# The late chunks' vector, scalar and Pool work in the source's order, transposes one slot later, and the second projection's weights in two arrays

## The chip, the cores and the metric

One core of one Trainium2 chip runs the kernel. The metric is the device time of one execution in microseconds. Before the change it is 664.35 us, the median of three runs (664.12 to 664.52).

## The reference

A banded attention with a linear position bias, followed by a two-layer feed-forward net without residual. B = 4, H = 8, S = 768, D = 64; a query sees 8 global keys and the 96 keys up to itself. q, k and v are float32, the two weights float64.

```python
scores = scale * np.matmul(q, k.transpose(0, 1, 3, 2))
keep = is_global | is_local                  # pos < 8, or 0 <= rel < 96
bias = -slopes[:, None, None] * dist[None, :, :]
scores = np.where(keep, scores + bias[None, :, :, :], -1000000000.0)
a = np.exp(scores - np.max(scores, axis=-1, keepdims=True))
a = a / (np.sum(a, axis=-1, keepdims=True) + 1e-09)
x = np.matmul(a, v)                          # then [B, S, H*D] -> 3072 x 512
h = x @ w_in                                 # 512 -> 2048
g = np.maximum(0.01 * h, h)
return (g @ w_out).astype(np.float32)        # 2048 -> 512
```

## The kernel before

**Tiling.** The 3072 tokens are 24 steps of 128. The attention of a step is two *units* of four heads each, 48 units in all. The feed-forward net takes *chunks* of steps: two of three steps, then nine of two (`CHUNKS`). Every float32 factor of the net is kept as a high part, rounded to TensorE's fp32r, and a remainder; each product is three matmuls (high x high, high x low, low x high). `copy` to fp32r on ACT makes the high part (`gh`, L511), a subtraction on DVE the low one (`gl`, L513).

**An attention unit** passes through *events*. Event t runs on TensorE the product with v of unit t-2 (L346) and the scores of unit t (L205). ACT copies the former from PSUM (`x`, L352), Pool splits it into the net's input. DVE adds the bias and takes the row's extreme (L219), ACT takes the exponential with its row sum (L232), DVE adds 1e-9 to the sum and inverts it (`rs`, L253 and L254), ACT scales the rows by it (L261). From unit 14 on the probabilities are then turned without TensorE (`turn`, L274): a DVE transpose of 32 x 32 blocks in place (L278), a DMA to a DRAM tile `via` (L243), and four DMAs back into `pt_d` (L245), all issued on the sync queue SP. Event t+2 reads `pt_d`.

**The early part** works through chunks 0 and 1 with attention events and the conversion of the weights between them. **The late loop** (L671 to L688) does the other nine chunks in 72 slots, eight for each chunk, a slot being a pair of the 16 blocks of 128 hidden units. In slot s stand, as written: the events of the slot (in slots 0, 1, 3 and 5 of eight, four for each chunk: those of the following chunk), `hidden_pair(s)` (24 matmuls, L491), `gates(s)`, `turn` of the slot's units, and `out_pair(s-2)`, the second projection of two slots ago (L542). `gates` copies the hidden pair from PSUM (`t`, L502), issues the fetch of a weight tile of the first projection for slot s+2 into a ring of two (`ring`, L479, on ACT's queue; it must wait until the tile's last reader is done), takes the leaky maximum (L504), makes the four block sums of a seven-product scheme (L507), and `gh` and `gl`; in the first chunks it also prepares the scheme's sums of `wout` (`prepare`, L523 and L601). From the third late chunk on (`SEVEN`) seven of a chunk's eight slots, all but the first, run with seven products in place of eight. At a chunk's end `results` copies three PSUM banks (L567, L572, L573), combines them on DVE (L523) and stores two rows of 128 x 512.

The hidden pair of odd slots uses the bank `ps_p`; its second half is also one of the four output banks (L666), so that the next output pair waits for the copy of `t`.

**What sets the order.** TensorE's instructions always keep the order of the source (`keep_in_program_order`). Those of DVE, ACT and Pool do so where `pin` is called while `pinned[0]` is true; `pinned[0] = j < half + NF` (L632) leaves it false at the end of the early part, so in the late loop these three engines are ordered by the scheduler, which simulates a time line (L1027) and takes what it deems ready. DMA issues on SP and on ACT's queue are left to the scheduler everywhere.

Of the kernel before, what the change touches and what calls it, by code (L numbers as in the profile page):

```python
# [11 lines left out]
F32R = mybir.dt.float32r  # L12
# [6 lines left out]
P = 128  # L19
# [33 lines left out]
def fast_path(ctx, tc, qp, kp, vp, wi, wo, nvec, nmall, out, B, H, S):  # L53
    nc = tc.nc
    NB = S // P
    DM = H * D
    NK = DM // P
    NF = wi.shape[0]
# [5 lines left out]
    GT = P * PAIR  # L64
# [3 lines left out]
    ring = ctx.enter_context(tc.tile_pool(name="ring", bufs=RING))  # L68
    win.update({2 * n + 1: ring.tile([P, 2, NK, P], F32R, name="ring") for n in range(RING)})
    outer = ctx.enter_context(tc.tile_pool(name="outer", bufs=1))  # L70
    wout = outer.tile([P, NF, 2, DM], F32R, name="wout")

    const = ctx.enter_context(tc.tile_pool(name="const", bufs=1))
    raw = ctx.enter_context(tc.tile_pool(name="raw", bufs=2))
# [41 lines left out]
    pinned = [True]  # L116
# [8 lines left out]
    def conversion(p):  # L125

        m, f = pieces[p]
        to = wout[:, f] if m else win[f]
        dh, dl = to[:, 0], to[:, 1]
        load_piece(p + STAGES - 1)  # L130
        scale, shift, low, *parts = split_float64(tc, pin, stage, staged.pop(p), dh, dl)
        due.extend(parts)
        return scale, shift, low

    units = {}
    NUNIT = NSTEP * NU
# [112 lines left out]
    def sums(u):  # L249
        d = units[u]  # L250
        sm = d.pop("sm")
        rs = att.tile([P, 16], F32, name="rs")[:, :4]
        pin(nc.vector.tensor_scalar(out=rs, in0=sm, scalar1=1e-9, scalar2=None, op0=ALU.add))  # L253
        pin(nc.vector.reciprocal(out=rs, in_=rs))  # L254
        if u >= BY_DVE:
            pr = d["pr"]
            for a in range(2):
                for j in range(2):
                    p, n = head(u, pr, a, j), 2 * a + j
                    if late.get("a"):  # L260
                        pin(nc.scalar.activation(out=p, in_=p, func=AF.Copy, scale=rs[:, n:n + 1]))  # L261
                    else:
                        pin(nc.vector.tensor_scalar(out=p, in0=p, scalar1=rs[:, n:n + 1], scalar2=1.0, op0=ALU.mult,
                                                    op1=ALU.mult))
            if not late.get("a"):
                turn(u)
            return

        dg = kept_rows.tile([P, 4, HALF], F32, name="dg")
        pin(nc.gpsimd.tensor_tensor(out=dg, in0=eye.unsqueeze(1).to_broadcast([P, 4, HALF]),  # L270
                                    in1=rs.unsqueeze(2).to_broadcast([P, 4, HALF]), op=ALU.mult))
        d["dg"] = dg
# [94 lines left out]
        pin(copy_exact(nc.gpsimd, xh, x))  # L367
        pin(nc.gpsimd.tensor_tensor(out=xl, in0=x, in1=xh.bitcast(F32), op=ALU.subtract))

    def event(t, conv=()):  # L370

        now, mid, old = t < NUNIT, t - 1 in units, t - 2 in units
        if t < LEAD + 2:

            av = (ps_lead if t % 2 else ps_x).tile([P, 2, 512], F32, tag="ps_av", name="ps_sc")
            scores(t, av)
            if mid:
                transposes(t - 1)
            if old:
                ov = ps_lead.tile([P, 2, 512], F32, tag="ps_ov", name="ps_ov")  # L380
                attn_v(t - 2, ov)
        else:

            ov = av = ps_x.tile([P, 2, 512], F32, tag="ps_av", name="ps_av")
            attn_v(t - 2, ov)
            if now:
                scores(t, av)
            if mid:
                transposes(t - 1)
            keep_x(t - 2, ov)  # L390
        if t + 2 < NUNIT:
            load_qk(t + 2)
        if t < NUNIT:
            load_v(t)
        if t < STAGES - 3:
            load_piece(t + 2)
        ends = due[:]
        due.clear()
        if ends:
            ends[0]()  # L400
        scale, shift, low = conversion(conv[0]) if conv else [lambda: None] * 3
        scale()
        if now:
            biased(t, av)
            exps(t)
        if ends:
            ends[1]()
        shift()
        if now:
            sums(t)  # L410
        low()
        if mid:
            keep_pt(t - 1)
        if old and t < LEAD + 2:
            keep_x(t - 2, ov)
        if old:
            split_x(t - 2)
# [10 lines left out]
    def ffn2(j):  # L428
        c, f = order[j]
        gh, gl = gts.pop(j)  # L430
        first = j == 0 or order[j - 1][0] != c
        last = j + 1 == len(order) or order[j + 1][0] != c
        if first:
            acc[c] = [ps_o.tile([P, DM], F32, tag="ps_o", name="ps_o") for _ in range(CHUNKS[c])]
        for tt in range(CHUNKS[c]):
            project(tc, acc[c][tt], wout[:, f], gh, gl, tt, first, last)
        if not last:
            return
        o = acc.pop(c)
        for tt in range(CHUNKS[c]):  # L440
            if f < NF - 1:
                kept.append(kept_rows.tile([P, DM], F32, name="kept", bufs=CHUNKS[c]))
                pin(nc.scalar.copy(out=kept[-1], in_=o[tt]))
                continue
            if c == 0:
                ob = kept[tt]
                nc.vector.tensor_tensor(out=ob, in0=o[tt], in1=ob, op=ALU.add)
            else:
                ob = stage.tile([P, DM], F32, tag="stage", name="part", bufs=STAGES)
                if tt % 2:  # L450
                    nc.vector.tensor_copy(out=ob, in_=o[tt])
                else:
                    nc.scalar.copy(out=ob, in_=o[tt])
            r0 = (first_step[c] + tt) * P
            nc.sync.dma_start(out=out[r0:r0 + P, :], in_=ob)
# [70 lines left out]
        return bank[1 + n // 2][:, n % 2 * GT:(n % 2 + 1) * GT]  # L526

    def block(f, n):
        return tuple(wout[:, f, y, n * GT:(n + 1) * GT] for y in range(2))

    def out_pair(s):

        c, p = at(s)
        gh, gl, a0 = pair.pop(s)

        def times(o, a, bh, bl, first, last, wide=None):
            a -= a0
            for n, (x, y) in enumerate(((gh, bh), (gh, bl), (gl, bh))):
                to = o
                if n == 0 and wide is not None:  # L540
                    to, y = wide
                tc.keep_in_program_order(nc.tensor.matmul(to, lhsT=x[:, a], rhs=y, start=first and n == 0,  # L542
                                                          stop=last and n == 2))
        e, o = 2 * p, 2 * p + 1
        end = s % NP == NP - 1
        if not fast(c, p):
            for n, f in enumerate((e, o)):
                for tt in range(PAIR):
                    times(bank[3 + tt], 2 * n + 1 - tt, wout[:, f, 0], wout[:, f, 1], p + n == 0, end and n == 1)
        else:  # L550
            h, l = sides[p]
            first = p == NP - 1
            t1, t2, t3 = ((h[:, i * GT:(i + 1) * GT], l[:, j * GT:(j + 1) * GT]) for j, i in enumerate((0, 1, 3 if first else 2)))
            for n, a, (bh, bl) in ((0, 5, t2), (1, 1, block(e, 0)), (3, 6, t3), (2, 4, t1), (4, 3, block(o, 0)),
                                   (6, 2, block(e, 1)), (5, 7, block(o, 1))):
                wide = None
                if first and n in (0, 3):
                    wide = bank[1 + n // 2], h[:, (1 + n // 3) * GT:(3 + n // 3) * GT]
                times(half_bank(n), a, bh, bl, wide is not None, end and n in (1, 2, 5, 6), wide)
        if end:  # L560
            results(c)
# [69 lines left out]
    for j in range(len(order)):  # L631
# [36 lines left out]
    sums_at = {2 + n: three[2 * n:2 * n + 2] for n in range(6)}  # L668
    sums_at.update({NP + n: [x] for n, x in enumerate(
        [(3, 0), (3, 1), (7, 3), (6, 3), (5, 3), (4, 3), (3, 2), (3, 3)] + [(p, n) for p in (2, 1) for n in range(4)])})  # L670
    for s in range(NS + 2):  # L671
        for t in ev_pair.get(s, ()):
            event(t)
        if s < NS:
            hidden_pair(s)
        if s == 0:
# [4 lines left out]
            nc.gpsimd.memset(late["w"].tile([P, 16], F32, tag="gap", name="gap"), 0.0)  # L681
        if s < NS:
            gates(s, sums_at.get(s, ()))
        for t in ev_pair.get(s, ()):
            if s and t < NUNIT:
                turn(t)
        if s >= 2:
            out_pair(s - 2)  # L688

# [207 lines left out]
def general_ffn(tc, wi, wo, xs, out):  # L897
# [4 lines left out]
    with ExitStack() as ctx:  # L902
# [14 lines left out]
        with tc.For_i(0, xv.shape[0], 1) as c:  # L917
# [7 lines left out]
            for f in range(NF):  # L925
                gh, gl = hidden(tc, lambda ins: None, work, ps_h, win[:, f], xh, xl, CT)
                for tt in range(CT // P):
                    project(tc, o[:, tt, :], wout[:, f], gh, gl, tt, f == 0, f == NF - 1)
            ob = work.tile([P, CT // P, DM], F32, name="hob")
            nc.scalar.copy(out=ob, in_=o)  # L930
            nc.sync.dma_start(out=ov[bass.ds(c, 1)].rearrange("o (t p) m -> p (o t) m", p=P), in_=ob)
# [25 lines left out]
def project(tc, o, w, gh, gl, tt, first, last):  # L957
    nc = tc.nc
    ts_ = slice(tt * P, (tt + 1) * P)
    tc.keep_in_program_order(nc.tensor.matmul(o, lhsT=gh[:, ts_], rhs=w[:, 0], start=first, stop=False))  # L960
    tc.keep_in_program_order(nc.tensor.matmul(o, lhsT=gh[:, ts_], rhs=w[:, 1], start=False, stop=False))  # L961
    tc.keep_in_program_order(nc.tensor.matmul(o, lhsT=gl[:, ts_], rhs=w[:, 0], start=False, stop=last))  # L962


def tile_kernel(tc, a, out, B, H, S):
# [65 lines left out]
```

## Time and profile before

| | |
|---|---|
| median of three runs | 664.35 us |
| profiled execution | 665.65 us, its span 663.8 us |
| mean granted TensorE clock | 0.977 |
| busy, share of the span | PE 94%, DVE 69%, ACT 52%, POOL 14% |
| waits of ps_p for the copy of t (L542 on L502) | 10.2 us in five waits, the longest 3.9 |
| via, from issue to landing | 3.3 us, 30 transfers |
| pt_d, from issue to landing | 3.5 us, 120 transfers |
| kr, vr, ring, from issue to landing | 4.0, 3.5, 3.4 us |

The page gives for each line of the kernel the busy time of its instructions and the idle time of their engine just before them, with what ended it. A busy TensorE is not TensorE at its peak: the granted clock stands in a row of its own. Timelines list single instructions with their start and length. In them `SPq` and `ACTq` are issues of transfers, whose landing is shown apart. Idle time of an engine that is not waited for costs nothing.

### The profile page before, as it was taken

How to read it: one execution, taken by the hardware profiler on the slowest of the kernel's cores; microseconds unless marked ns; L12 is line 12 of the kernel's file. 1: busy time of each engine (PE TensorE's matmuls, PEld its weight loads, DVE VectorE, ACT ScalarE, POOL GpSimd, SP SyncE). 2: the span in 40 equal slices, each digit the busy share in tenths (PEclk: the TensorE clock that was granted, in tenths of full speed). 3: DMA queues.
4: the chain of work that ended last, by engine and by line, in shares of the span. 5: the costliest groups of instructions: out<-in, count | busy, mean ns of one | idle time of the engine just before them, and what ended most of it. 6: DMA issues, size and time to landing. Idle time of an engine off the chain costs nothing.

```text
span 663.8 us, 16802 instructions
## 1 busy us (share of the span) xinstructions
PE 620.7 (94%) x6536; PEld 569.5 (86%) x6536; DVE 458.2 (69%) x1286; ACT 348.1 (52%) x902; POOL 89.9 (14%) x150
## 2 busy tenths in 40 slices
PE   5679999999999899799979999999999999999993
PEld 4569889998888788689979999999999999999993
DVE  5979988886656974865686676765766766744653
ACT  5877854444444645444545744754664664522321
POOL 3435700000201001000011110110010010110000
PEclk9789999999999999999979999999999999999998
DMA  7775744432547665644745676765765774733311
GB/s 278 242 284 190 222 160 157 157 127 81 166 160 252 206 186 154 201 166 152 242 144 171 192 260 206 213 214 176 231 223 196 227 229 151 229 104 96 127 64 38
DMA packets 63335, 120.71 MB, mean 182 GB/s; under 512 B 8976, under 2 KB 28432, under 8 KB 63248
## 3 DMA queue, kind: packets, MB, share of 16 engines
q1 hardware_dynamic: 53168, 82.86, 38.7%
q10 hardware_dynamic: 10080, 36.70, 16.7%
q8 instruction: 53, 0.87, 0.6%
q14 instruction: 34, 0.28, 0.1%
HBM read 96.21 MB, written 23.33 MB: 180 GB/s over the span
## 4 chain that ended last, share of the span: by engine, by line
PE 75%; DVE 11%; ACT 5%; DMA 4%; issue 2%; POOL 1%; SPq 0%; ACTq 0%; DVEq 0%; POOLq 0%
PE ps_m L542 19%; PE ps_h L491 13%; PE ps_p L491 13%; PE ps_p L542 6%; PE ps_av L346 4%; PE ps_av L205 3%; ACT pr L232 3%; PE ps_h L940 3%; PE ps_h L942 3%; PE ps_o L960 3%; PE ps_o L961 3%; PE ps_h L941 3%; PE ps_o L962 3%; DVE wk L523 3%; DMA out_dram<-part 1%
## 5 line engine op out<-in xcount | busy, mean ns | idle before, releaser
L511 ACT CAST gh<-t 128x896 fp32r<-128x896 f32 (+1 forms) x72 | 61.9, 859 | 100.1 <-DVE t L507 54.9
L513 DVE TENSOR_TENSOR gl<-t,gh 128x896 fp32r<-128x896 f32 (+1 forms) x72 | 70.6, 981 | 52.0 <-ACT gh L511 51.9
L232 ACT ACTIVATE pr<-pr,nmall 128x192 f32<-128x192 f32 (+1 forms) x192 | 83.3, 437 | 23.7 <-DVE nmall L219 23.5
L49 POOL TENSOR_SCALAR xh<-x 128x256 fp32r<-128x256 f32 x48 | 28.6, 596 | 453.4 <-ACT x L352 370.6
L542 PE MATMUL ps_m<-wout,gh 128*128 128x256 f32 (+1 forms) x394 | 86.9, 302 | 0.0
L504 DVE SCALAR_TENSOR_TENSOR t<-t 128x512 f32<-128x512 f32 x72 | 49.7, 690 | 41.1 <-ACT t L502 40.5
L542 PEld LDWEIGHTS ps_m<-wout,gh 128*128 128x128 f32 x394 | 61.7, 189 | 1.9
L542 PE MATMUL ps_m<-wout,gl 128*128 128x256 f32 (+1 forms) x197 | 59.6, 303 | 0.5 <-DVE gl L513 0.5
L491 PE MATMUL ps_p<-xh,win 128*128 128x256 f32 x288 | 58.2, 287 | 0.0
L491 PE MATMUL ps_h<-xh,win 128*128 128x256 f32 x288 | 58.1, 286 | 0.0
L491 PE MATMUL ps_h<-xh,ring 128*128 128x256 f32 x288 | 56.4, 281 | 0.0
L542 PE MATMUL ps_p<-wout,gh 128*128 128x256 f32 (+1 forms) x182 | 46.3, 336 | 10.3 <-ACT t L502 10.2
L491 PE MATMUL ps_p<-xh,ring 128*128 128x256 f32 x288 | 55.1, 277 | 0.0
L507 DVE TENSOR_TENSOR t<-t 128x128 f32<-128x128 f32 x212 | 52.0, 285 | 2.7
L491 PEld LDWEIGHTS ps_p<-xh,win 128*128 128x128 f32 x288 | 46.3, 188 | 5.9 <-issue 5.7
L219 DVE CUSTOM_DVE_ANT_0 pr<-ps_av,nbw 128x192 f32<-128x192 f32 x136 | 40.3, 352 | 15.7 <-ACT x L352 15.6
L491 PEld LDWEIGHTS ps_h<-xh,win 128*128 128x128 f32 x288 | 47.7, 193 | 2.5 <-issue 2.2
L491 PEld LDWEIGHTS ps_h<-xh,ring 128*128 128x128 f32 x288 | 47.1, 191 | 0.0
L491 PEld LDWEIGHTS ps_p<-xh,ring 128*128 128x128 f32 x288 | 46.2, 188 | 0.0
L542 PE MATMUL ps_m<-h,gh 128*128 128x256 f32 (+1 forms) x159 | 46.1, 290 | 0.0
L261 ACT ACTIVATE pr<-pr,rs 128x192 f32<-128x192 f32 (+1 forms) x116 | 42.5, 438 | 4.0 <-DVE rs L254 3.0
L542 PEld LDWEIGHTS ps_p<-wout,gh 128*128 128x128 f32 x182 | 30.4, 191 | 16.4 <-ACT t L502 13.5
(145 smaller groups left out, 1648.0 us busy)
## 6 DMA issues: line engine op xcount, KB each, us to landing
ring<-wd ACTq DMA_DIRECT2D x70, 512.0 KB, 3.4
via<-pr SPq DMA_DIRECT2D x30, 384.0 KB, 3.3
pt_d<-via SPq DMA_DIRECT2D x120, 96.0 KB, 3.5
kr<-in_kp_dram SPq DMA_DIRECT2D x40, 256.0 KB, 4.0
vr<-in_vp_dram SPq DMA_DIRECT2D x40, 256.0 KB, 3.5
wst<-in_wi_dram SPq DMA_DIRECT2D x16, 512.0 KB, 3.7
wst<-in_wo_dram SPq DMA_DIRECT2D x16, 512.0 KB, 3.8
qs<-in_qp_dram SPq DMA_DIRECT2D x24, 256.0 KB, 4.6
```

Source lines behind the costliest of these rows:

```text
L49: return eng.tensor_scalar(out=dst, in0=src, scalar1=1.0, scalar2=1.0, op0=ALU.mult, op1=ALU.mult)
L205: tc.keep_in_program_order(nc.tensor.matmul(own(u, av[qf, j, a * KW:(a + 1) * KW]), lhsT=q[rows, a, qf], rhs=keys(rows, a, f), start=True, ...
L219: pin(nc.vector.tensor_tensor_reduce(out=head(u, pr, a, j), in0=own(u, ps[:, j, a * KW:(a + 1) * KW]), in1=nb, scale=-0.125, scalar=3.0e38 ...
L232: pin(nc.scalar.activation(out=p, in_=p, func=AF.Exp, scale=-1.0, bias=nm[:, 2 * a + j:2 * a + j + 1], accum_out=sm[:, 2 * a + j:2 * a + j ...
L261: pin(nc.scalar.activation(out=p, in_=p, func=AF.Copy, scale=rs[:, n:n + 1]))
L346: tc.keep_in_program_order(nc.tensor.matmul(av[out, a, cols], lhsT=v[rows, t, j, :], rhs=near(rows, j, t, fs), start=(n == 0), stop=(n == ...
L491: tc.keep_in_program_order(nc.tensor.matmul(o, lhsT=w[:, y, k], rhs=x[:, k, :], start=(k + i == 0), stop=(k == NK - 1 and i == 2)))
L504: pin(nc.vector.scalar_tensor_tensor(out=g, in0=g, scalar=0.01, in1=g, op0=ALU.mult, op1=ALU.max))
L507: pin(nc.vector.tensor_tensor(out=t[:, o], in0=t[:, x], in1=t[:, y], op=op))
L511: pin(nc.scalar.copy(out=gh[:, :n - a0], in_=t[:, a0:n]))
L513: pin(nc.vector.tensor_tensor(out=gl[:, :n - a0], in0=t[:, a0:n], in1=gh[:, :n - a0].bitcast(F32), op=ALU.subtract))
L542: tc.keep_in_program_order(nc.tensor.matmul(to, lhsT=x[:, a], rhs=y, start=first and n == 0, stop=last and n == 2))
```

## The change

Three things. `pinned[0]` is set to true ahead of the late loop, so that DVE, ACT and Pool follow the source there. `event` no longer computes the sums in the late loop; after `gates(s)` the loop first turns the units of the *previous* slot and then computes the sums and the scaling of this slot's. And `wout`, one array with high and low parts side by side, becomes two arrays `woh` and `wol`, with the functions that read it adapted. The test `"a" in late` takes the place of `late.get("a")`.

```diff
     ring = ctx.enter_context(tc.tile_pool(name="ring", bufs=RING))
     win.update({2 * n + 1: ring.tile([P, 2, NK, P], F32R, name="ring") for n in range(RING)})
     outer = ctx.enter_context(tc.tile_pool(name="outer", bufs=1))
-    wout = outer.tile([P, NF, 2, DM], F32R, name="wout")
+    wout = [outer.tile([P, NF, DM], F32R, name=name) for name in ("woh", "wol")]
 
     const = ctx.enter_context(tc.tile_pool(name="const", bufs=1))
     raw = ctx.enter_context(tc.tile_pool(name="raw", bufs=2))
...
     def conversion(p):
 
         m, f = pieces[p]
-        to = wout[:, f] if m else win[f]
-        dh, dl = to[:, 0], to[:, 1]
+        dh, dl = (x[:, f] for x in wout) if m else (win[f][:, y] for y in range(2))
         load_piece(p + STAGES - 1)
         scale, shift, low, *parts = split_float64(tc, pin, stage, staged.pop(p), dh, dl)
         due.extend(parts)
...
             for a in range(2):
                 for j in range(2):
                     p, n = head(u, pr, a, j), 2 * a + j
-                    if late.get("a"):
+                    if "a" in late:
                         pin(nc.scalar.activation(out=p, in_=p, func=AF.Copy, scale=rs[:, n:n + 1]))
                     else:
                         pin(nc.vector.tensor_scalar(out=p, in0=p, scalar1=rs[:, n:n + 1], scalar2=1.0, op0=ALU.mult,
                                                     op1=ALU.mult))
-            if not late.get("a"):
+            if "a" not in late:
                 turn(u)
             return
 
...
         pin(copy_exact(nc.gpsimd, xh, x))
         pin(nc.gpsimd.tensor_tensor(out=xl, in0=x, in1=xh.bitcast(F32), op=ALU.subtract))
 
-    def event(t, conv=()):
+    def event(t, conv=(), whole=True):
 
         now, mid, old = t < NUNIT, t - 1 in units, t - 2 in units
         if t < LEAD + 2:
...
         if ends:
             ends[1]()
         shift()
-        if now:
+        if now and whole:
             sums(t)
         low()
         if mid:
...
         if first:
             acc[c] = [ps_o.tile([P, DM], F32, tag="ps_o", name="ps_o") for _ in range(CHUNKS[c])]
         for tt in range(CHUNKS[c]):
-            project(tc, acc[c][tt], wout[:, f], gh, gl, tt, first, last)
+            project(tc, acc[c][tt], [x[:, f] for x in wout], gh, gl, tt, first, last)
         if not last:
             return
         o = acc.pop(c)
...
         return bank[1 + n // 2][:, n % 2 * GT:(n % 2 + 1) * GT]
 
     def block(f, n):
-        return tuple(wout[:, f, y, n * GT:(n + 1) * GT] for y in range(2))
+        return tuple(x[:, f, n * GT:(n + 1) * GT] for x in wout)
 
     def out_pair(s):
 
...
         if not fast(c, p):
             for n, f in enumerate((e, o)):
                 for tt in range(PAIR):
-                    times(bank[3 + tt], 2 * n + 1 - tt, wout[:, f, 0], wout[:, f, 1], p + n == 0, end and n == 1)
+                    times(bank[3 + tt], 2 * n + 1 - tt, *(x[:, f] for x in wout), p + n == 0, end and n == 1)
         else:
             h, l = sides[p]
             first = p == NP - 1
...
     sums_at = {2 + n: three[2 * n:2 * n + 2] for n in range(6)}
     sums_at.update({NP + n: [x] for n, x in enumerate(
         [(3, 0), (3, 1), (7, 3), (6, 3), (5, 3), (4, 3), (3, 2), (3, 3)] + [(p, n) for p in (2, 1) for n in range(4)])})
+    pinned[0] = True
+    turns = []
     for s in range(NS + 2):
-        for t in ev_pair.get(s, ()):
-            event(t)
+        events = ev_pair.get(s, ())
+        for t in events:
+            event(t, whole=False)
         if s < NS:
             hidden_pair(s)
         if s == 0:
...
             nc.gpsimd.memset(late["w"].tile([P, 16], F32, tag="gap", name="gap"), 0.0)
         if s < NS:
             gates(s, sums_at.get(s, ()))
-        for t in ev_pair.get(s, ()):
-            if s and t < NUNIT:
-                turn(t)
+        for t in turns:
+            turn(t)
+        turns = [t for t in events if t < NUNIT]
+        for t in turns:
+            sums(t)
         if s >= 2:
             out_pair(s - 2)
 
...
 def project(tc, o, w, gh, gl, tt, first, last):
     nc = tc.nc
     ts_ = slice(tt * P, (tt + 1) * P)
-    tc.keep_in_program_order(nc.tensor.matmul(o, lhsT=gh[:, ts_], rhs=w[:, 0], start=first, stop=False))
-    tc.keep_in_program_order(nc.tensor.matmul(o, lhsT=gh[:, ts_], rhs=w[:, 1], start=False, stop=False))
-    tc.keep_in_program_order(nc.tensor.matmul(o, lhsT=gl[:, ts_], rhs=w[:, 0], start=False, stop=last))
+    tc.keep_in_program_order(nc.tensor.matmul(o, lhsT=gh[:, ts_], rhs=w[0], start=first, stop=False))
+    tc.keep_in_program_order(nc.tensor.matmul(o, lhsT=gh[:, ts_], rhs=w[1], start=False, stop=False))
+    tc.keep_in_program_order(nc.tensor.matmul(o, lhsT=gl[:, ts_], rhs=w[0], start=False, stop=last))
 
 
 def tile_kernel(tc, a, out, B, H, S):
```

In the new kernel the lines named above stand one line higher (L502 is L501, L278 is L277, and so on). TensorE and Pool keep their order. DVE, in slots 40 and 41, the first two of the sixth late chunk, before the change; `pr_6288` and `rs_6298` belong to the unit of slot 40, `pr_6395` and `rs_6405` to that of slot 41, `t_6334` and `t_6438` to their gates:

```order
L253 TENSOR_SCALAR rs_6298<-sm_6293 128x4
L254 RECIPROCAL rs_6298<-rs_6298 128x4
L504 SCALAR_TENSOR_TENSOR t_6334<-t_6334 128x512
L278 STREAM_TRANSPOSE pr_6288<-pr_6288 128x768
L513 TENSOR_TENSOR gl_6340<-t_6334,gh_6339 128x512
L219 ISA pr_6395,nmall_71<-ps_av_6372,nbw_152 128x2x96
...
L253 TENSOR_SCALAR rs_6405<-sm_6400 128x4
L254 RECIPROCAL rs_6405<-rs_6405 128x4
L504 SCALAR_TENSOR_TENSOR t_6438<-t_6438 128x512
L507 TENSOR_TENSOR t_6438<-t_6438 128x128 x3
L278 STREAM_TRANSPOSE pr_6395<-pr_6395 128x768
L507 TENSOR_TENSOR t_6438<-t_6438 128x128
```

DVE at the same place after the change; `pr_6289` and `rs_6337` belong to the unit of slot 40, `pr_6388` and `rs_6445` to that of slot 41, `t_6328` and `t_6424` to their gates:

```order
L503 SCALAR_TENSOR_TENSOR t_6328<-t_6328 128x512
L512 TENSOR_TENSOR gl_6334<-t_6328,gh_6333 128x512
L252 TENSOR_SCALAR rs_6337<-sm_6294 128x4
L253 RECIPROCAL rs_6337<-rs_6337 128x4
L218 ISA pr_6388,nmall_71<-ps_av_6365,nbw_153 128x2x96
...
L503 SCALAR_TENSOR_TENSOR t_6424<-t_6424 128x512
L506 TENSOR_TENSOR t_6424<-t_6424 128x128 x4
L512 TENSOR_TENSOR gl_6434<-t_6424,gh_6433 128x896
L277 STREAM_TRANSPOSE pr_6289<-pr_6289 128x768
L252 TENSOR_SCALAR rs_6445<-sm_6393 128x4
L253 RECIPROCAL rs_6445<-rs_6445 128x4
```

The transpose of slot 40's unit moves from ahead of `gl` of slot 40 to behind `gl` of slot 41, and the sum and its inverse move from ahead of the leaky maximum to behind `gl` of the same slot.

ACT at the same place before the change:

```order
L502 COPY t_6334<-ps_h_6309 128x512
L479 DMA ring_6336<-wd_125 128x1024
L261 ACTIVATE pr_6288<-pr_6288,rs_6298 128x2x96 x4
L511 CAST gh_6339<-t_6334 128x512
L352 COPY x_6389<-ps_av_6372 128x256
L232 ACTIVATE pr_6395,sm_6400<-pr_6395,nmall_71 128x2x96 x4
L502 COPY t_6438<-ps_p_2689 128x512
L479 DMA ring_6440<-wd_125 128x1024
L261 ACTIVATE pr_6395<-pr_6395,rs_6405 128x2x96 x4
L567 COPY part_6480<-ps_m_2692 128x512
L572 COPY u_6483<-ps_m_2690 128x256
L573 COPY part_6481<-ps_p_2689 128x512
```

And after it:

```order
L501 COPY t_6328<-ps_h_6303 128x512
L478 DMA ring_6330<-wd_126 128x1024
L510 CAST gh_6333<-t_6328 128x512
L260 ACTIVATE pr_6289<-pr_6289,rs_6337 128x2x96 x4
L351 COPY x_6382<-ps_av_6365 128x256
L231 ACTIVATE pr_6388,sm_6393<-pr_6388,nmall_71 128x2x96 x4
L501 COPY t_6424<-ps_p_2690 128x512
L478 DMA ring_6426<-wd_126 128x1024
L510 CAST gh_6433<-t_6424 128x896
L478 DMA ring_6515<-wd_126 128x1024
L260 ACTIVATE pr_6388<-pr_6388,rs_6445 128x2x96 x4
L566 COPY part_6473<-ps_m_2693 128x512
```

The four scalings change places with `gh` in both slots, `gh` of slot 41 stands ahead of the three copies of the finished chunk (the first of them is the last row shown), and the ring fetch for slot 44, whose tile the hidden pair of slot 42 still reads, now stands ahead of the scalings of slot 41.

More of the change, by code (lines that the diff above doesn't have):

```diff
@@ L927, in general_ffn @@
                 for tt in range(CT // P):
-                    project(tc, o[:, tt, :], wout[:, f], gh, gl, tt, f == 0, f == NF - 1)
+                    project(tc, o[:, tt, :], [wout[:, f, y] for y in range(2)], gh, gl, tt, f == 0, f == NF - 1)
             ob = work.tile([P, CT // P, DM], F32, name="hob")
```

## The prediction

> **What bounds the kernel now.** The views were read in this order: busy times, TensorE's waits, the stretch table, the chain that ended last, the timelines of single engines. Busy time and waits (line waited for: us in total, times, longest), and one steady stretch of 40 us:
>
> ```profile
> PE 620.7 (94%) x6536; PEld 569.5 (86%) x6536; DVE 458.2 (69%) x1286; ACT 348.1 (52%) x902; POOL 89.9 (14%) x150
> PE ps_p L542 <- ACT t L502: 10.2, 5, 3.9
> PE ps_av L346 <- DMA pt_d<-via: 1.7, 1, 1.7
> 540.00:580.00 40.00, 40.00 (x461) 37.85 (x461) 26.41 (x78) 22.27 (x56) 3.47 (x6) 1.00 0.60 191
> ```
>
> PE bounds the kernel; from the fourth late chunk on it has no gap at all (40.00 of 40.00 us, granted clock 1.00). In the late slots it loses 10.2 us in five waits for the copy of ps_p. Two of these are followed by a halved clock (stretch, its us, busy by engine, clock; then pieces of the chain; then one timeline row):
>
> ```profile
> 281.71:285.13 3.42, 3.42 (x11) 2.67 (x10) 2.12 (x6) 1.18 (x4) 0.00 (x0) 0.50 0.62 229
> 336.33:343.15 6.82, 5.67 (x26) 5.67 (x27) 5.81 (x18) 3.21 (x11) 0.00 (x0) 0.50 0.36 127
> ```
> ```profile
> 243.75 0.69 PE ps_m L542 x3
> ...
> 282.49 1.28 PE ps_m L542 x3
> ...
> 339.13 4.69 PE ps_h L491 x24
> ```
> ```profile
> 337.49 0.79 PE L542 MATMUL ps_p<-wout,gh 128*128 128x256 f32 x2 [3.72 <-ACT t L502]
> ```
>
> Three matmuls took 1.28 us instead of 0.69 and 24 took 4.69 instead of 2.73 (row below). After the 3.9 us pause three such groups lost 0.6 each, 1.8 in all; after the 3.72 us pause the hidden pair lost 1.9 and the rest of the output pair about 0.8. So the late slots hold 10.2 + 4.5 = **14.7 us** that a better order could win, and no more.
>
> **The steady chunk.** Slots 40 to 43 stand for every chunk: events fall in slots 0, 1, 3, 5 of eight, and the event of slot 3 needs the probabilities of slot 0's event. PE's chain:
>
> ```profile
> 468.30 0.49 PE ps_av L346 x16
> ...
> 469.44 3.02 PE ps_p L491 x24
> 472.47 1.77 PE ps_m L542 x15
> 474.24 0.35 PE ps_p L542 x3
> ...
> 474.94 2.73 PE ps_h L491 x24
> 477.68 0.69 PE ps_m L542 x3
> ...
> 480.43 0.83 PE ps_av L346 x32
> ```
>
> Slot 41 begins at 468.30, its hidden pair ends at 472.47, slot 42's at 477.68, and slot 43 reads pt_d at 480.43. From the end of hidden pair 41 to that read PE has 7.96 us of work. The other engines there:
>
> ```profile
> 466.58 1.50 ACT L261 ACTIVATE pr<-pr,rs 128x192 f32<-128x192 f32 x4
> 468.22 0.62 ACT L511 CAST gh<-t 128x512 fp32r<-128x512 f32 x1
> 469.56 0.37 ACT L352 COPY x<-ps_av 128x256 f32<-128x256 f32 x1 [0.73 <-PE ps_av L205]
> ...
> 472.05 0.19 ACT L232 ACTIVATION_READ_ACCUMULATOR pr<-pr,nmall 128x1 f32 x1
> 472.51 0.59 ACT L502 COPY t<-ps_p 128x512 f32<-128x512 f32 x1 [0.27 <-PE ps_p L491]
> ...
> 474.98 0.59 ACT L567 COPY part<-ps_m 128x512 f32<-128x512 f32 x1 [0.49 <-PE ps_m L542]
> 475.46 0.38 ACT L572 COPY u<-ps_m 128x256 f32<-128x256 f32 x1
> 475.73 0.61 ACT L573 COPY part<-ps_p 128x512 f32<-128x512 f32 x1
> 476.20 0.97 ACT L511 CAST gh<-t 128x896 fp32r<-128x896 f32 x1
> ```
> ```profile
> 466.10 0.17 DVE L253 TENSOR_SCALAR rs<-sm 128x4 f32<-128x4 f32 x1 [1.10 <-ACT pr L232]
> ...
> 468.11 0.98 DVE L278 STREAM_TRANSPOSE pr<-pr 128x768 f32<-128x768 f32 x1 [0.85 <-ACT pr L261]
> 469.01 0.65 DVE L513 TENSOR_TENSOR gl<-t,gh 128x512 fp32r<-128x512 f32 x1
> ...
> 473.12 0.69 DVE L504 SCALAR_TENSOR_TENSOR t<-t 128x512 f32<-128x512 f32 x1 [0.47 <-ACT t L502]
> 473.85 0.70 DVE L507 TENSOR_TENSOR t<-t 128x128 f32<-128x128 f32 x3
> ...
> 477.25 1.09 DVE L513 TENSOR_TENSOR gl<-t,gh 128x896 fp32r<-128x896 f32 x1
> ```
>
> Before, slot 40's transpose runs at 468.11, ahead of slot 41. The trip that follows it on the sync queue (issue times, then us from issue to landing min/median/max, first of pt_d, then of via):
>
> ```profile
> 341.49 0.33 SPq L243 DMA_DIRECT2D via<-pr  x1
> 343.84 1.75 SPq L245 DMA_DIRECT2D pt_d<-via  x4
> ```
> ```profile
> 469.28 0.38 SPq L243 DMA_DIRECT2D via<-pr  x1
> ...
> 472.93 1.75 SPq L245 DMA_DIRECT2D pt_d<-via  x4
> ```
> ```profile
> DMA to landing us min/median/max: 1.9/3.4/6.1
> ```
> ```profile
> DMA to landing us min/median/max: 2.0/3.2/4.9
> ```
>
> A trip is via, then the last of four issues (1.75 less one issue of 0.42, so 1.3 us), then pt_d. By medians 3.2 + 1.3 + 3.4 = 7.9 us; between 2.0 + 1.3 + 1.9 = 5.2 and 4.9 + 1.3 + 6.1 = 12.3. At 341.49, with no load issued inside the trip, via took 2.35, which with 1.3 and 3.4 makes 7.1. The new order too has no load between via and pt_d in this trip, but a ring fetch runs beside it; I take the middle, **7.6**.
>
> **The change, part by part.** *Two weight arrays* cost nothing: PE's order and shapes stay, and its matmuls read the same rows.
>
> *The new wait, slot 43.* By the new DVE order slot 40's transpose stands behind gl of slot 41. Step by step: gh of slot 40 ends at 468.84 as before, gl 0.65 gives 469.5, the sum and reciprocal 0.4 give 469.9, the four scalings 1.5 give 471.4. ACT now has the copy of x behind them: 471.8 instead of 469.93, and bias and exponentials keep their distance to it. So the copy of ps_p starts not at 472.24 (end of the last read of the accumulator) but at 474.1, and ends at 474.7; PE needs it at 474.24, a small stall of 0.5. Then leaky 0.7, four adds 1.0 (three took 0.70), gh 0.97, gl 1.09, transpose 0.98: 479.5. The trip lands at 479.5 + 7.6 = 487.1, against 480.43: **6.7 us late**.
>
> *What is late meanwhile.* The scalings of slot 41 wait for a sum that now stands behind the transpose (479.9), so they end at 481.4, and the three copies of the finished chunk's banks, queued behind them on ACT, begin only then, not at 474.98. Output pair 40 rewrites those banks: PE waits from about 478.2 to 482.0 for the first copy, works 2.8 us to 484.8, and waits for pt_d the remaining 2.3. This lies inside the 6.7, and makes a floor: even a trip of 5.2 us leaves PE at 484.8, 4.4 late. With a trip of 12.3 it is 11.4.
>
> It happens once for each chunk that still brings events, eight times: 8 x 6.7 = **+53.6** (35 to 91).
>
> *The clock.* PE pauses about 4 us and then 2 us each time; the two pauses of 3.7 and 3.9 us above cost 1.8 and 2.7 by the halved clock. A part falls into the second wait and is hidden, so I take 1.5 of a possible 0 to 2.7: 8 x 1.5 = **+12** (0 to 22). The Trainium skill (TensorE: Matmul & The Clock Gate, What's actually happening) says that the clock halves after at least one idle window of about 3.4 us and recovers after a busy one of that length; by it every such pause would cost half a window, 1.7 us, which would make an estimated 13.6 in place of 12, and the two stretches of 3.42 and 6.82 us above agree with that grid.
>
> *What is removed.* The five waits came from wk work and biases that DVE took out of the source's order; in slots 11 and 19, where the 3.9 and 3.72 stand, PE will now be late for pt_d and the copy will long be done. I count all **-14.7**.
>
> *New small stalls in chunks that still prepare weights.* In slot 4, DVE has behind the hidden pair: copy 0.6, leaky 0.7, six preparations, gl 0.65, two remainders, transpose 0.98, and slot 5's bias queues behind all of it. Preparation pieces cost (mean ns after the comma):
>
> ```profile
> L523 DVE TENSOR_TENSOR wk<-wout 128x256 f32<-128x256 f32 x42 | 16.8, 415 | 3.1 <-DMA out_dram<-kept 2.8 <-DMA out_dram<-part 0.2
> ```
>
> Eight at 0.415 are 3.3, the whole 6.2 us, against about 4.7 of PE's output pair, event and the copy of x. The 1.5 us reach PE less the 0.7 of three matmuls that need no copy; slots 9 and 13 are alike, in 11 and 19 the preparation also waits for a result's store. Six slots at about 1.2: **+7** (0 to 12).
>
> Sum: -14.7 + 53.6 + 12 + 7 = **+57.9**. The profiled span of 663.8 becomes 721.7 (its execution took 665.65, so 723.5), and the median of the runs, 664.35, becomes **722**.
>
> **Rivals.** *A quick trip, chance 0.16.* The stall ends at its floor because DMA has little else to carry while PE stands, and the clock recovers inside the waits: 8 x 4.4 = 35, small stalls 4, less 14.7, gives 689. For it: via took 2.0 at its quickest. Against: the medians come from the same traffic. [...]
>
> *A vicious circle, chance 0.12.* The clock halves for two windows each time (2.7), trips take 9 us, and slot 5's event, whose pt_d issues stand behind a load that waits for slot 8, is late by 1 as well: 8 x (8.1 + 2.7 + 1) + 7 - 14.7 = +86.7, 751.
>
> *The other side: the trip is hidden, chance 0.05.* PE comes to slot 43 no earlier than pt_d, because DVE's source order ends the early waits and nothing takes their place: 664.35 - 14.7 = 650. It decides once transpose to landing takes under 480.43 - 479.5, 0.9 us; the quickest row is 5.2. Only a transpose that runs earlier than I read could do that.
>
> *No effect, chance 0.03.* The new order is nearly neutral since a wait of DVE that I missed already held transposes back: 664. Against it: before, the transpose ran at 468.11, ahead of slot 41's bias.
>
> **How the numbers follow.** My forecast, 722, has 0.64; its own range is 705 to 740. With the quick and the long case the range of 8 in 10 is **692 to 748**. Faster by over 0.2% (1.3 us, about what this kernel's runs can tell) 0.05, within it 0.03, slower 0.92.
>
> **What would show it.** Right: TensorE's waits list ps_av on pt_d eight times with some 2 us or more each, and ps_m on the copy of part seven or eight times with about 4; the wait of ps_p for t falls below 10 us; the granted clock dips once a chunk, so that PEclk shows 7s and 8s through the late half; the transposes of slots 1, 9, 17 start about 11 us later against their hidden pair than now. Wrong: pt_d waits under 1 us, or transposes ahead of gl. If the time is right but the clock stays at 1.00, the trip was longer than 7.6.

## The result and the profile after

The change made the kernel slower: 716.38 us median of four runs (713.99 to 722.23) against 664.43 us (664.12 to 666.49), a ratio of 1.0788 with a 95% interval of 1.0712 to 1.0864. The profiled execution has a span of 712.1 us, 48.3 more than before.

Busy times on the page of the changed kernel, then TensorE's waits there (line waited for: us in total, times, longest):

```profile
PE 637.6 (90%) x6536; PEld 578.0 (81%) x6536; DVE 459.8 (65%) x1282; ACT 346.3 (49%) x906; POOL 89.6 (13%) x150
```
```profile
PE ps_m L541 <- ACT part L566: 23.3, 7, 3.8
PE ps_p L541 <- ACT t L501: 13.4, 17, 3.0
PE ps_av L345 <- DMA pt_d<-via: 7.3, 6, 4.5
```

These three rows hold 44.0 us; the rows of ps_p and pt_d of before held 11.9. So waits account for 32.1 of the 48.3 us, and 16.9 are TensorE's own busy time, which rose from 620.7 (the other waits fell by some 0.7). The largest wait is not the one for `pt_d`, it is the one for the copy of a finished chunk's bank.

One steady chunk, from the event of slot 41 to that of slot 49, in the stretch table of before and then of after (stretch, its us, busy by engine with counts, granted clock, share and GB/s of the transfers). The third row is the stretch of half clock inside the second:

```profile
468.23:516.61 48.38, 48.38 (x529) 45.95 (x528) 32.72 (x96) 27.61 (x72) 5.33 (x8) 1.00 0.67 217
```
```profile
495.42:551.50 56.08, 51.59 (x528) 47.94 (x527) 32.48 (x96) 26.94 (x71) 5.85 (x8) 0.97 0.57 183
509.15:512.56 3.41, 3.41 (x9) 2.64 (x10) 3.23 (x8) 1.01 (x3) 0.00 (x0) 0.50 0.38 102
```

The same work takes 56.08 us in place of 48.38, 7.7 more. Where it goes is to be seen on ACT, DVE, SP's queue and TensorE around the end of the chunk, in the timeline of the changed kernel (start, us, operation, idle time before it and its releaser):

```profile
498.67 0.35 ACT L351 COPY x<-ps_av 128x256 f32<-128x256 f32 x1
501.22 0.56 ACT L501 COPY t<-ps_p 128x512 f32<-128x512 f32 x1
503.65 0.94 ACT L510 CAST gh<-t 128x896 fp32r<-128x896 f32 x1 [1.87 <-DVE t L506]
505.65 0.33 ACTq L478 DMA_DIRECT2D ring<-wd  x1
506.96 1.49 ACT L260 ACTIVATE pr<-pr,rs 128x192 f32<-128x192 f32 x4 [2.37 <-DVE rs L253]
508.36 0.56 ACT L566 COPY part<-ps_m 128x512 f32<-128x512 f32 x1
```
```profile
504.63 1.09 DVE L512 TENSOR_TENSOR gl<-t,gh 128x896 fp32r<-128x896 f32 x1 [1.06 <-ACT gh L510]
505.64 0.97 DVE L277 STREAM_TRANSPOSE pr<-pr 128x768 f32<-128x768 f32 x1
506.69 0.18 DVE L253 RECIPROCAL rs<-rs 128x4 f32<-128x4 f32 x1
```
```profile
506.67 0.33 SPq L242 DMA_DIRECT2D via<-pr  x1
510.07 1.75 SPq L244 DMA_DIRECT2D pt_d<-via  x4
```
```profile
508.98 0.66 PE L541 MATMUL ps_m<-woh,gh 128*128 128x512 f32 x1 [3.36 <-ACT part L566]
...
513.52 0.71 PE L345 MATMUL ps_av<-pt_d,vr 64*64 64x128 f32 x6
```

Slot 40's transpose stands behind `gl` of slot 41 (505.64), slot 41's sum behind that (506.69), slot 41's scalings wait 2.37 us for the sum, and the copy of `part` stands behind them on ACT (the ring fetch that stands ahead of the scalings was issued at 505.65, before the sum was ready at 506.87, and held nothing up): it runs from 508.36, and TensorE, which wanted the bank at 505.62, begins at 508.98. Output pair 40 then runs mostly at half clock and takes 4.6 us, where it took 2.9 before (477.51 to 480.43). That is just long enough for `pt_d`, issued from 510.07 on and landed whole at 513.75, to be there for its reads from 513.52 on. So two late things end within 0.3 us of each other in this chunk: the copy with the slower work behind it, and `pt_d`.

### The profile page after: what moved, and what is told of

It reads as the page before. It is cut to its first block, busy times and chain, and to the rows that moved or that the text cites. A ratio compares the mean times of both kernels' runs of the same rounds, so it can differ in the third digit from the quotient of the medians.

```text
span 712.1 us, 16803 instructions
## 1 busy us (share of the span) xinstructions
PE 637.6 (90%) x6536; PEld 578.0 (81%) x6536; DVE 459.8 (65%) x1282; ACT 346.3 (49%) x906; POOL 89.6 (13%) x150
## 4 chain that ended last, share of the span: by engine, by line
PE 48%; DVE 20%; ACT 17%; DMA 8%; issue 4%; POOL 1%; SPq 1%; ACTq 1%; DVEq 0%; POOLq 0%
PE ps_m L541 10%; PE ps_h L490 6%; PE ps_p L490 6%; ACT pr L231 5%; ACT gh L510 4%; PE ps_p L541 4%; DVE gl L512 4%; ACT pr L260 4%; DVE t L506 3%; PE ps_h L944 3%; DVE t L503 3%; PE ps_h L946 3%; PE ps_o L964 3%; PE ps_o L965 3%; PE ps_o L966 3%
## 5 line engine op out<-in xcount | busy, mean ns | idle before, releaser
L541 PE MATMUL ps_m<-woh,gh 128*128 128x256 f32 (+1 forms) x197 | 62.3, 316 | 23.3 <-ACT part L566 23.3
L260 ACT ACTIVATE pr<-pr,rs 128x192 f32<-128x192 f32 (+1 forms) x120 | 44.0, 437 | 47.2 <-DVE rs L253 41.7
L541 PE MATMUL ps_m<-woh,gl 128*128 128x256 f32 (+1 forms) x197 | 61.9, 314 | 0.0
L541 PE MATMUL ps_m<-wol,gh 128*128 128x256 f32 (+1 forms) x197 | 61.7, 313 | 0.0
L541 PEld LDWEIGHTS ps_m<-woh,gh 128*128 128x128 f32 x197 | 38.2, 194 | 25.9 <-ACT part L566 24.7
L490 PE MATMUL ps_h<-xh,win 128*128 128x256 f32 x288 | 56.6, 281 | 0.0
L541 PE MATMUL ps_p<-woh,gh 128*128 128x256 f32 (+1 forms) x91 | 34.3, 377 | 13.5 <-ACT t L501 13.4
```

Of the source, the lines that this page charges most:

```text
L490: tc.keep_in_program_order(nc.tensor.matmul(o, lhsT=w[:, y, k], rhs=x[:, k, :], start=(k + i == 0), stop=(k == NK - 1 and i == 2)))
```

## The experiments

Each kernel was timed against the kernel before in three rounds or more. The ratios are to the kernel before. Their line numbers differ from the changed kernel's by up to five.

**The parts of the change.** First, the two arrays alone: the late loop and `event` as before, `wout` as in the change.

```diff
-    wout = outer.tile([P, NF, 2, DM], F32R, name="wout")
+    wout = [outer.tile([P, NF, DM], F32R, name=name) for name in ("woh", "wol")]
```

> Only the two weight arrays of the change; the late loop, the place of the sums and the free order of DVE, ACT and Pool as before. My theory (the time is lost in the order alone): 664.4 us, within 0.3%, waits as before. Rival (the arrays' new addresses slow the matmuls or their weight loads): over 670, with a longer mean of the second projection's rows at clock 1.00.

665.02 us, 1.0007 (0.9982 to 1.0032). The arrays cost nothing that can be measured.

Second, everything but the line that pins:

```diff
-    pinned[0] = True
     turns = []
```

> All of the change but the line that pins the late loop: sums behind gates and transposes a slot later in the source, the three engines ordered by the scheduler. Its order puts the transpose of slot 40 back ahead of gl of slot 40. My theory: 666 us, between 662 and 671. Rival (the later place in the source costs by itself, through the transfers' order on SP): 700 or more.

665.04 us, 1.0001 (0.9982 to 1.0020). With the same source the scheduler puts transposes and sums back where they were: in slots 40 to 47 DVE and ACT run the same operations in the same order as before. Here the place in the source does nothing until the order is fixed.

Third, pinned, but with sums and transposes where the source of before had them:

```diff
     pinned[0] = True
-    turns = []
...
-        events = ev_pair.get(s, ())
-        for t in events:
-            event(t, whole=False)
+        for t in ev_pair.get(s, ()):
+            event(t)
...
-        for t in turns:
-            turn(t)
-        turns = [t for t in events if t < NUNIT]
-        for t in turns:
-            sums(t)
+        for t in ev_pair.get(s, ()):
+            if s and t < NUNIT:
+                turn(t)
```

> The two arrays and the pinned order, but sums inside the event and the transpose behind gl of its own slot, as the source before had it. My theory (the place of sums and transposes is what costs): no wait for the copy of part over 1 us, no wait for pt_d beyond the one of before; the scalings now stand ahead of the copy of t in event slots, so ps_p waits some 0.5 us three times a chunk, about 12 us in all, with 5 for the preparing chunks: 672 us, between 660 and 682. Rival (the pinned order as such costs, whatever the source says): 700 or more.

718.50 us, 1.0809 (1.0772 to 1.0846): as slow as the change, by another wait. TensorE's waits and the one in slot 41, then ACT and DVE in slot 41 of that kernel:

```profile
PE ps_p L541 <- ACT t L501: 47.3, 22, 4.1
508.65 0.39 PE L541 MATMUL ps_p<-woh,gh 128*128 128x256 f32 x1 [2.21 <-ACT t L501]
```
```profile
506.64 1.49 ACT L260 ACTIVATE pr<-pr,rs 128x192 f32<-128x192 f32 x4 [0.51 <-DVE rs L253]
508.04 0.56 ACT L501 COPY t<-ps_p 128x512 f32<-128x512 f32 x1
```
```profile
503.00 0.97 DVE L277 STREAM_TRANSPOSE pr<-pr 128x768 f32<-128x768 f32 x1
503.90 0.32 DVE L218 CUSTOM_DVE_ANT_0 pr<-ps_av,nbw 128x192 f32<-128x192 f32 x1
...
506.17 0.17 DVE L252 TENSOR_SCALAR rs<-sm 128x4 f32<-128x4 f32 x1 [1.10 <-ACT pr L231]
```

No wait for the copy of `part` and none for `pt_d`, as the theory had it. But the chain bias, exponential, sum, scalings now stands whole ahead of the copy of `t`: TensorE waits 2.21 us here where 0.5 was expected, since `gl` and the transpose of slot 40 also delay the bias (503.90, though the copy of `x` that it follows was done at 502.64) and the sum waits 1.10 for the last exponential. The expectation of 672 was wrong by 46 us, and the theory had to be put more sharply: not only the change's places are bad, the old source's are as well. What was good before was what the scheduler had made of it.

**A fixed order close to the scheduler's.** If that is so, a pinned kernel with the scheduler's places of sums, scalings and transposes in slots 40 and 41 written into the source must be as fast as before. It is called the woven kernel from here on. In `gates`, `mine` being the units of this slot:

```diff
         pin(nc.scalar.copy(out=g, in_=ps))
         fetch(s + RING)
+        for u in mine:
+            sums(u)
         pin(nc.vector.scalar_tensor_tensor(out=g, in0=g, scalar=0.01, in1=g, op0=ALU.mult, op1=ALU.max))
...
+        for u in mine:
+            turn(u)
         pin(nc.scalar.copy(out=gh[:, :n - a0], in_=t[:, a0:n]))
```

> Pinned as in the change, but the source written so that DVE and ACT stand as the scheduler had them before in slots 40 and 41: the sum, its inverse and the scalings right behind the copy of t, the transpose of the same slot ahead of gh and gl. Theory (where the sums and transposes stand decides, not that the order is fixed): the steady chunks run without a wait as before; the preparing chunks keep up to 10 us of waits for t in place of the 14.7 of before: 660 us, between 652 and 672. Rival (a fixed order costs whatever it is): over 695, with waits for t in every chunk as in the pinned order with the sums inside the event.

653.76 us, 0.9876 (0.9844 to 0.9907): 1.2% faster than the kernel before, with the whole interval below 1. The wait for `t`, and the same steady chunk from the event of slot 41 to that of slot 49, in the waits and the stretch table of this kernel, then two rows of ACT in slot 41:

```profile
PE ps_p L545 <- ACT t L501: 3.3, 3, 1.4
```
```profile
455.50:503.90 48.40, 48.40 (x528) 45.95 (x527) 33.20 (x96) 27.66 (x72) 5.24 (x8) 1.00 0.69 218
```
```profile
462.27 0.94 ACT L514 CAST gh<-t 128x896 fp32r<-128x896 f32 x1 [0.47 <-PE ps_m L545]
463.12 0.58 ACT L570 COPY part<-ps_m 128x512 f32<-128x512 f32 x1
```

The steady chunk takes 48.40 us, where it took 48.38 before. A fixed order as such costs nothing; where sums and transposes stand decides. The place of `gh`, which the change also moved, does not: here too it stands ahead of the copies of `part`. What is gained lies in the three preparing chunks, where the free order had its five waits of 10.2 us for `t`; here three of 3.3 are left, and no stretch of half clock while the late loop's matmuls run. From the hidden pair of slot 0 to that of slot 24 this kernel takes 155.3 us in place of 165.3, and from there to that of slot 64 239.7 in place of 239.9. In the preparing chunks its order is far from the scheduler's (about 32 of DVE's 92 operations in slots 8 to 15 stand elsewhere, 5 of 80 in slots 40 to 47), so the gain is not the scheduler's order made fixed; which of its moves there brings it was not tested.

**The two moves apart.** In the woven kernel the transposes alone are moved, to the next slot behind its `gl`:

```diff
-        for u in mine:
-            turn(u)
         a0 = n // 8
...
+        late_turns = turns
         turns = [t for t in events if t < NUNIT]
         if s < NS:
             gates(s, sums_at.get(s, ()), turns)
+        for t in late_turns:
+            turn(t)
```

And in the change the transposes are moved back to their own slot, behind its sums. That leaves the sums late, and the transposes only as late as they must be, since they need the scaled rows:

```diff
-        for t in turns:
-            turn(t)
         turns = [t for t in events if t < NUNIT]
         for t in turns:
             sums(t)
+        for t in turns:
+            turn(t)
```

> The woven order with one edit: the transpose stands a slot later, behind gl of the next slot, as in the change; the sums and scalings stay right behind the copy of t. Theory (the late transposes alone make pt_d late, whatever the sums do): slot 40's transpose moves from 455.7 to about 463.3 us on the woven kernel's own time line, its trip of 7.1 lands at 471.4, and slot 43 reads at 467.67: eight waits for pt_d of about 3.8 us, each followed by 3.4 us or more of halved clock worth 1.7; no wait for the copy of part over 1 us. 654 + 44 = 698 us, between 685 and 712. Rival (the late sums are what costs, the transpose has room): 660 us or less.

> The change with one edit: the transpose follows the sums in the same slot, so only the sums' place behind gl is left of the move. Theory: DVE waits for the scalings before the transpose, and slot 41's bias stands behind it, so the copy of ps_p comes about 1.9 us late in slot 41; the copies of part stand behind slot 41's scalings and come 2 to 2.5 us late; pt_d is in time. 654 + 8 x 4.3 and some 8 for the clock = 697 us, between 680 and 712. Rival (the late transposes are all that costs): 660 us or less.

Transposes late alone: 715.98 us, 1.0779 (1.0750 to 1.0808). Sums late alone: 704.88 us, 1.0619 (1.0591 to 1.0646). Waits of the first kernel and the one in slot 43, its DVE and SP queue at slots 41 to 43, then the waits of the second:

```profile
PE ps_av L345 <- DMA pt_d<-via: 25.8, 9, 6.8
PE ps_av L345 <- DVE pr L277: 15.5, 3, 5.2
510.35 0.65 PE L345 MATMUL ps_av<-pt_d,vr 64*64 64x128 f32 x2 [5.10 <-DMA pt_d<-via]
```
```profile
501.76 0.97 DVE L277 STREAM_TRANSPOSE pr<-pr 128x768 f32<-128x768 f32 x1
```
```profile
502.80 0.33 SPq L242 DMA_DIRECT2D via<-pr  x1
505.14 0.95 SPq L584 DMA_DIRECT2D out_dram<-part  x2
507.69 1.75 SPq L244 DMA_DIRECT2D pt_d<-via  x4
```
```profile
PE ps_p L541 <- ACT t L501: 20.9, 17, 3.3
PE ps_m L541 <- ACT part L566: 17.0, 7, 2.9
```

Either move alone costs nearly what both cost together: 62 us over the woven kernel for the transposes, 51 for the sums, 63 for the change, which has both. They stall TensorE at the same place, the end of a chunk, one in slot 42 and one in slot 43, so the one hides the other.

(In the first kernel's waits the second row names a transpose, but it is `pt_d` as well: its three reads, at 396.49, 453.60 and 567.15, begin 0.13 us after the second of their four pieces of `pt_d` landed, as the read at 510.35 begins 0.14 after. The transpose named is that of another unit, which happened to end at about that time.)

With the transposes late, the trip from slot 40's transpose on took 8.5 us, not the 7.1 expected, because `via` took 4.87; the waits of the steady chunks are 5.1 to 5.5 us in place of 3.8, and the total missed its range by 4 us. With the sums late, six of the seven waits for the copy of `part` took 2.5 to 2.9 us, a little over the 2 to 2.5 expected, and the total lies in its range.

**Each edit on the change itself.** The results ahead of the sums:

```diff
-        for t in turns:
-            sums(t)
         if s >= 2:
             out_pair(s - 2)
+        for t in turns:
+            sums(t)
```

The previous slot's transposes ahead of the gates:

```diff
+        for t in turns:
+            turn(t)
         if s < NS:
             gates(s, sums_at.get(s, ()))
-        for t in turns:
-            turn(t)
```

And both of these edits in one kernel.

> The change with one edit: the sums and scalings stand behind the output pair and its results, so the three copies of a finished chunk come ahead of the scalings on ACT. My theory: the seven waits of 3.4 us for the copy of part go, and pt_d, which lands at the same time as now, becomes the wait of the same place: seven or eight waits of about 5.3 us, clock pauses as before, 714 us, between 705 and 722. Rival (the copy alone is the cause, pt_d is only dragged along): 23 us of waits and about 13 us of halved clock go, 680 us, pt_d waits under 1 us each.

> The change with one edit: the transposes of the previous slot's unit stand ahead of the slot's gates on DVE, not behind. Theory (two causes end at the same place, the copy of part by the queue on ACT and pt_d by the late transpose): pt_d waits go, and the wait for the copy of part stays, shorter by the transpose's 0.97 us: seven of about 2.4 us; with less halved clock 700 us, between 690 and 710. Rival (the late transpose is the whole cause): both waits go, 680 us or less.

> Both edits: transposes ahead of the gates, sums and scalings behind the results. Theory: both waits at the end of a chunk go (30 us) with most of the 17 us of halved clock; the bias of slot 43's event now stands behind a later gl of slot 42, which leaves a wait for t of about 1 to 2 us a chunk: 680 us, between 665 and 695. Rival (either edit alone already shows all there is to win): no better than the better of the two.

Results first: 725.89 us, 1.0922 (1.0882 to 1.0963). Transposes first: 700.60 us, 1.0566 (1.0539 to 1.0594). Both: 695.98 us, 1.0490 (1.0456 to 1.0523). The waits of the three, in this order, with one read in slot 43 of the first:

```profile
PE ps_av L345 <- DMA pt_d<-via: 20.1, 9, 5.9
PE ps_av L345 <- DVE t L506: 18.8, 4, 4.8
520.94 1.23 PE L345 MATMUL ps_av<-pt_d,vr 64*64 64x128 f32 x21 [0.57 <-DMA pt_d<-via]
```
```profile
PE ps_m L541 <- ACT part L566: 16.8, 7, 2.8
PE ps_p L541 <- ACT t L501: 15.0, 18, 2.6
PE ps_av L345 <- DMA pt_d<-via: 2.5, 2, 2.0
```
```profile
PE ps_p L541 <- ACT t L501: 20.3, 22, 3.6
PE ps_av L345 <- DMA pt_d<-via: 13.6, 11, 2.0
```

With the results first, the copy of `part` is no longer waited for at all, and `pt_d` takes its place with 38.9 us (the second row again is `pt_d`: its four reads begin 0.13 to 0.24 us after the second of their pieces landed, and in slot 43 the read at 520.94 then waits for the last piece): the direction that the theory gave, but 12 us above its 714 and 4 above its range. The stall is now one long pause, behind which the clock is halved for 6.83 us in most chunks: 58.0 us of half clock in the late loop in place of 37.5, which can cost 10 of the 12 us. The rival, that the copy alone is the cause, would have shown 680 and falls.

Transposes first took the waits for `pt_d` away from the second late chunk on and left seven of 2.4 us on average for the copy, as forecast, at 700.6 where 700 was expected.

Both edits together were forecast at 680 and reached only 696, one us beyond the range: `pt_d` is waited for again, 1.4 to 3.0 us in each of the last five chunks that bring events, and `t` 20.3 us in all. In slot 43 of that kernel the trip from slot 40's transpose on took 9.5 us and landed at 497.01, and TensorE stood ready from 494.81. With the transposes first alone the same trip took 9.2 us, but there TensorE was still busy with the output pair that the copy had held up. Why these trips take longer than the changed kernel's 7.1 is not shown. None of these kernels keeps the sums behind `gl` and loses the stall.

## Why the prediction came out right, point by point

The predicted 722 us (692 to 748) stands against 716.4; its sum of +57.9 against 48.3 in the profile. The mechanism of slots 40 to 43 was as told, and the sizes of three terms were not. That the total came so near is in part luck: the new wait was put 24.7 us too high, and the clock with TensorE's other busy time 9.4 and the waits for `t` 6.4 too low.

**Step by step, slot 40 to 43.** The end of hidden pair 41 is 472.47 on the old time line and 499.83 on the new, 27.36 later. By that shift the predicted times become: transpose done 506.9 (measured 506.61), pause of TensorE from 505.6 to 509.4 (505.62 to 508.98), `pt_d` landed 514.5 (513.75, a trip of 7.14 us in place of 7.6). Each is within 0.8 us.

**The new wait, +53.6.** It was over-sized. The sum took the pause for the copy, 2.8 us of work at full clock and a second wait for `pt_d` that ended 6.7 us late. But the clock was halved in just these 2.8 us, which became 4.6, so the second wait disappeared behind slower work: from slot 32 on the changed kernel shows one `pt_d` wait of 0.2 us and no other. Measured, the two rows grew by 23.3 + 5.6 = 28.9 us. The prediction's own sign of failure, waits for `pt_d` under 1 us, came true in all but one slot, and its sign of being right, eight such waits of 2 us or more, did not. Yet the time held, because the pause it called a floor carries the stall, and `pt_d` lands only 0.2 us behind it. That it would have bound next was shown by the kernel with the results first. Two other signs came as told: seven waits for the copy of `part`, of 2.5 to 3.8 us, and dips of the clock in seven of the eight chunks.

**The clock, +12, less the 4.5 counted as removed.** It was under-sized. The late loop of the changed kernel has eight stretches of half clock of 3.41 or 6.83 us, 37.5 us in all, against 10.2 before. At half clock half of the time is lost, so the difference is up to 13.7 us, where 7.5 net were predicted. The busy time grew by 16.9; where the rest, some 3 us, comes from is not shown. Wait and clock together were 8.2 us for a chunk by the prediction. Measured from the end of hidden pair 41, 27.36 us later than before, to the start of hidden pair 43 at 515.36, 33.52 later, they were 6.2 (the chunk's 7.7 holds small waits of other slots too). So a part of the loss was put under the wait and stood under the clock, and 2 us a chunk were not there.

**The waits removed, -10.2, and the small ones added, +7.** Here the prediction was wrong. The waits of `ps_p` did not fall to 7, they went from 10.2 to 13.4 us, in 17 places. The 3.9 and 3.7 us of slots 11 and 19 went, as told, but slots 2, 5 and 21 now have waits of 3.0, 1.6 and 2.7, where they had none, 1.3 and 0.8. So the preparing chunks hold 9.7 us, nearly what they held before. The rest are 0.2 to 0.8 us, up to twice in a steady chunk, of which the prediction had named one, without a term in its sum.

**The two arrays** cost nothing, as said. **The rivals**: the quick trip (689), the hidden trip (650) and no effect fell; the floor that the quick trip rested on is what the steady chunk shows, with more clock lost than that case allowed. The circle (751) fell too: in the changed kernel the ten trips from slot 40 on took 6.7 to 8.4 us with a middle of 7.15, not 9.

## What to carry to other kernels

Before an order is fixed, read off what order the scheduler had been giving and write that into the source: fixing a bad order cost 8%, and fixing one close to the scheduler's cost the steady chunks nothing (48.40 us against 48.38). The 1.2% that it gained in all came in the preparing chunks, where the two orders differ most. A producer that is moved behind a slot's main work delays not only its own consumer but everything queued behind its next stage, here the bank copies on ACT behind the scalings. When two late things stop the same engine within a few us of each other, removing one shows far less than it costs, or even a loss: from the changed kernel one edit gained 16 us and the other lost 10, though from the woven kernel either move alone cost 51 us or more. Test them alone from a good state, not from the bad one.

## What the runs showed of the hardware

The clock halves after less than a full idle stretch. All dips in the late loops lie on a grid of 3.41 us within each run, so the late loops can be cut into stretches of that grid. In the eleven kernels of this case, 57 such stretches at full clock left TensorE idle for over 1.9 us by its records, and each was followed by a stretch of half clock. Of 15 with 1.6 to 1.9 us idle two were, and of 1390 with less none was. Two stretches near the border in one kernel (transposes and results both first), each with the stretch behind it:

```profile
440.22:443.64 3.42, 1.57 (x7) 0.94 (x5) 2.20 (x7) 1.06 (x4) 0.00 (x0) 1.00 0.96 294
443.64:447.05 3.41, 3.02 (x59) 2.66 (x60) 2.54 (x6) 1.15 (x4) 0.00 (x0) 1.00 0.42 151
494.84:498.25 3.41, 1.50 (x45) 1.32 (x48) 1.76 (x5) 1.96 (x5) 0.00 (x0) 1.00 0.78 239
498.25:501.66 3.41, 3.41 (x24) 2.87 (x16) 2.28 (x7) 1.21 (x2) 0.71 (x1) 0.50 0.68 200
```

TensorE's 1.57 us busy kept the clock at 1.00, and 1.50 us busy in the stretch from 494.84 brought 0.50. By these records the border is not sharp: in the kernel with the sums late 1.56 us busy, from 500.48, brought 0.50 too. So where a pause lies counts as well as its length. First the changed kernel, where the grid cuts a pause of 2.48 us that ends at 281.19, then the kernel with the sums late, where one of 2.58 us that ends at 448.92 lies inside one stretch:

```profile
277.05:280.46 3.41, 1.66 (x15) 1.46 (x13) 2.10 (x6) 1.28 (x4) 0.00 (x0) 1.00 0.36 108
280.46:283.87 3.41, 2.68 (x12) 2.17 (x12) 1.12 (x3) 1.16 (x3) 0.00 (x0) 1.00 0.96 308
```
```profile
445.87:449.28 3.41, 0.83 (x7) 0.58 (x6) 1.76 (x4) 2.38 (x7) 0.00 (x0) 1.00 0.45 161
449.28:452.69 3.41, 3.41 (x10) 2.65 (x9) 3.31 (x9) 0.83 (x2) 0.00 (x0) 0.50 0.32 120
```

The first pause cost no clock, the second was followed by a stretch at 0.50. The Trainium skill (TensorE: Matmul & The Clock Gate, What's actually happening) states a free-running window of about 3.4 us, which these traces bear out, but names a whole idle window as the condition for the half clock; here the measurement differs, and somewhat over half of one was enough.
